# Reordering the rows of a two-stage spectrum so that the real/imaginary exchange copies neighbouring partitions

## The chip, the core and the metric

The kernel runs on one core of one Trainium2 chip. The metric is device time in microseconds of one execution of the whole program. Beside it there is a profile of one execution: busy times of the engines (PE is TensorE, DVE is VectorE, ACT is ScalarE, POOL is GpSimd, SP is SyncE, which here only issues transfers), the DMA queues, and the waits between them.

## The reference

The inputs are bfloat16, one sequence of S = 2048 positions with D = 640 channels. The reference computes a gated long convolution beside a feed-forward block:

```
xn = layernorm(A_q)
kv = (4-tap causal filter of A_k with A_shift_k) * A_v
y  = causal convolution of kv with A_ssm_k along S, per channel   (in the reference by FFT of length 2S)
y  = y + kv * A_ssm_D
s  = xn * y
g  = silu(gelu(xn @ B_w1 + B_b1) @ B_w2 + B_b2)                  (inner width F = 1728)
out = A_q + s * g
```

## The kernel before

**The convolution** is done in the frequency domain with matmuls, in two stages each way. Position s is split as p (128 partitions) and n (16). Stage F1 (`k_f1`, `u_f1`, lines 429 and 442) multiplies each of the 16 slices n by a cosine and a sine matrix (`WA`, `WB`), so that 32 tiles of [128, 640] come out, 128 values r for each n and for each of c = 0, 1. They are stored to DRAM scratch (`k_store` and `u_store`, lines 439 and 449, issued on POOL) and read back in another order (`kin_load` line 479, `uin_load` line 515, issued on SP), so that one tile holds, on its 128 partitions, 4 values of r with all 16 n and both c. Stage F2 (`k_f2` line 482, `u_f2` line 523) multiplies such a tile by one 128x128 matrix `F2m`. What comes out are 32 groups g, each with 128 spectrum rows: 4 values of r, 16 frequencies n, and real or imaginary part c. For the filter the 32 groups are kept in SBUF as `Khat[:, g, :]`. For the signal they stay in PSUM as `mu`.

**The complex product** needs, beside the filter's row, the row with real and imaginary part exchanged. `swap_load(g2)` (line 518, step `mk`) makes it for two groups at a time: two transfers from SBUF to SBUF, issued on SP, copy one half of the spectrum rows of `Khat` onto the other half of the partitions of a ring slot, and back. Before the change c is the highest bit of the row number (row = 64 c + 16 r + n), so the halves are partitions 0 to 63 and 64 to 127. The ring is `Khat` rows 32 to 39, which is four slots of two groups. `product(g)` (line 526, step `mp`) is one VectorE instruction: it multiplies `mu` by `Khat[:, g]` and by the exchanged rows. `inv1` (line 533, step `mc`) turns both products back with the matrices `I1a` and `I1b`, `inv1_out` (`me`) evicts the result, `c_store` (`ms`, POOL) and `cab_load` (`yl`, SP) reorder it through DRAM, and `inv2` (`y`) finishes.

**The three small matrices** `F2m`, `I1a`, `I1b` are made on the chip. `small_iotas` (line 248, step `sp`) writes index vectors on POOL. `small_phase` (line 262, step `s`) takes index bits of the partition number with `bits()` (a bitwise AND and a cast, two VectorE instructions each) and builds phases and masks. `small_sine` (step `ss`) takes the sine on ACT, and `small_mats` (step `sm`) multiplies by the mask.

**The feed-forward block** is tiled by 512 positions (4 chunks): `ffn1` (step `h`, line 376) and `ffn2` (step `g`, line 394) on PE, evictions `he` (line 383) and `ge` on ACT.

**The order** of everything is written out by hand: `PLAN` (line 30) lists the steps, and each engine's instructions and each queue's transfers stand in that order. SP issues the loads `ml` and `mk` in the order of the plan: mk0, ml0, ml1, mk1, mk2, mk3, ml2, ml3, ml5, ml4, ml7, ml10, ml8, mk4, mk5, ml12, ml11, mk6, ml6, mk7, ml9, mk8 to mk10, ml14, ml15, mk11, ml13, mk12 to mk15. A load waits on SP until its ring slot is free, and what is behind it on SP waits too. Near the start, the plan has `sp s A0 h0 h1 P2 ee A1 P1 P0 pt pb he0 he1 h2`: the small phase, the first two `ffn1` groups, the parameter loads, the transposition of the biases (`pt`, line 506) and its eviction (`pb`, line 510), and then the first GELU, which needs the biases. PSUM has two buffers for the feed-forward block, so `h2` waits for `he0`.

Of the kernel before, what the change touches and what calls it, by code (L numbers as in the profile page):

```python
# [14 lines left out]
ALU = mybir.AluOpType  # L15

P = 128
# [57 lines left out]
def kernel(  # L75
# [15 lines left out]
    nc = tc.nc  # L91
# [49 lines left out]
    Khat = wts.tile([P, NG + NR, D], BF16, name="Khat")  # L141
# [65 lines left out]
    def scratch(shape, dtype):  # L207
        n = 1
        for d in shape:
            n *= d  # L210
        reg = next(r for r in regions if r[1] + n <= r[0].shape[1])
        o = reg[1]
        reg[1] += n
        v = reg[0][:, o:o + n]
        if dtype != F32:
            v = v.bitcast(dtype)
        if len(shape) == 2:
            v = v.rearrange("p (a b) -> p a b", a=shape[0])
        elif len(shape) == 3:
            v = v.rearrange("p (a b c) -> p a b c", a=shape[0], b=shape[1])  # L220
        return v
# [24 lines left out]
    sm = {}  # L246

    def small_iotas():
        kcol = scratch([1], I32)
        nc.gpsimd.iota(kcol, pattern=[[0, 1]], base=0, channel_multiplier=1)  # L250

        def grid(*pattern):
            g = scratch([P], F32)
            nc.gpsimd.iota(g, pattern=[list(p) for p in pattern], base=0, channel_multiplier=0,
                           allow_small_or_imprecise_dtypes=True)
            return g

        sm["f"] = grid([0, 8], [1, 16]), grid([8, 2], [0, 64]), grid([0, 2], [32, 4], [0, 16])
        sm["i"] = grid([0, 4], [2, 16], [0, 2]), grid([0, 64], [8, 2]), grid([16, 4], [0, 32])
        sm["kcol"] = kcol  # L260

    def small_phase():
        def bits(mask):
            i = scratch([1], I32)
            nc.vector.tensor_single_scalar(out=i, in_=sm["kcol"], scalar=mask, op=ALU.bitwise_and)
            f = scratch([1], F32)
            nc.vector.tensor_copy(out=f, in_=i)
            return f

        def stt(o, a, s, b, op0, op1):  # L270
            nc.vector.scalar_tensor_tensor(out=o, in0=a, scalar=s, in1=b, op0=op0, op1=op1)

        ph = scratch([3, P], F32)
        mask = scratch([3, P], F32)
        nf, cf, rf = bits(30), bits(1), bits(96)
        ni, ci, ri = bits(15), bits(64), bits(48)
        nm_f, cm_f, rm_f = sm["f"]
        nm_i, cm_i, rm_i = sm["i"]
        c8 = scratch([1], F32)
        nc.vector.tensor_single_scalar(out=c8, in_=cf, scalar=8.0, op=ALU.mult)  # L280
        c4 = scratch([1], F32)
        nc.vector.tensor_single_scalar(out=c4, in_=ci, scalar=0.25, op=ALU.mult)
        stt(ph[:, 0, :], nm_f, nf[:, 0:1], cm_f, ALU.mult, ALU.add)
        stt(ph[:, 2, :], nm_i, ni[:, 0:1], cm_i, ALU.mult, ALU.subtract)
        nc.vector.tensor_scalar(out=ph[:, 1, :], in0=ph[:, 2, :], scalar1=c4[:, 0:1], scalar2=None, op0=ALU.add)
        nc.vector.tensor_scalar(out=ph[:, 2, :], in0=ph[:, 2, :], scalar1=8.0, scalar2=None, op0=ALU.add)
        nc.vector.tensor_scalar(out=ph[:, 0, :], in0=ph[:, 0, :], scalar1=c8[:, 0:1], scalar2=None, op0=ALU.subtract)
        nc.vector.tensor_scalar(out=mask[:, 0, :], in0=rm_f, scalar1=rf[:, 0:1], scalar2=None, op0=ALU.is_equal)
        for i in (1, 2):
            nc.vector.tensor_scalar(out=mask[:, i, :], in0=rm_i, scalar1=ri[:, 0:1], scalar2=2.0 / 4096.0,  # L290
                                    op0=ALU.is_equal, op1=ALU.mult)
        q = scratch([3, P], I32)
        nc.vector.tensor_single_scalar(out=q, in_=ph, scalar=float(8 + 16 + 128), op=ALU.add)
        nc.vector.tensor_single_scalar(out=q, in_=q, scalar=31, op=ALU.bitwise_and)
        sm.update(q=q, sn=scratch([3, P], F32), mask=mask)
# [22 lines left out]
    def take(key, pool, shape, dtype, tag, bufs=None):  # L318
        if key not in live:
            live[key] = pool.tile(shape, dtype, tag=tag, name="%s%d" % key, **({"bufs": bufs} if bufs else {}))  # L320
        return live[key]
# [196 lines left out]
    def swap_load(g2):  # L518
        ks = take(("ks", g2), pools["ring"], None, None, "ks")
        for a in range(2):  # L520
            nc.sync.dma_start(out=ks[64 * a:64 * a + 64, :, :], in_=Khat[64 - 64 * a:128 - 64 * a, 2 * g2:2 * g2 + 2, :])

    def u_f2(g):
        mm2(big_of(("mu", g)), F2m, live["uin", g // 2][:, g % 2, :])
# [48 lines left out]
    def prologue():  # L573
# [92 lines left out]
        "h": ffn1, "he": ffn1_out, "g": ffn2, "ge": ffn2_silu, "gm": ffn2_mul, "ga": last_add, "gs": last_store,  # L666
        "w": f1_phase, "ws": f1_sines, "d": add_d, "em": tap3, "ee": tap3_out,
        "sp": small_iotas, "s": small_phase, "ss": small_sine, "sm": small_mats,
        "kt": k_tr, "kc": k_tr_out, "kf": k_f1, "ke": k_f1_out, "ks": k_store,
        "cv": kv_step, "uf": u_f1, "ue": u_f1_out, "us": u_store,  # L670
        "fl": kin_load, "ff": k_f2, "fe": k_f2_out, "it": i2_tr, "ie": i2_out,
        "ml": uin_load, "mk": swap_load, "mu": u_f2, "mp": product, "mc": inv1, "me": inv1_out, "ms": c_store,
        "q": xq_load, "yl": cab_load, "y": inv2, "yt": gate, "yo": out_add, "ys": out_store,
    }
# [35 lines left out]
```

## Time and profile before

| what | value |
|---|---|
| median of 3 runs | 231.27 us (229.96, 231.27, 231.30) |
| span of the profiled execution, first to last instruction | 231.0 us (no time of its own is listed beside it) |
| PE busy | 211.6 us, 92% |
| DVE busy | 184.1 us, 80% |
| ACT busy | 149.6 us, 65% |
| POOL busy | 43.1 us, 19% |
| the 32 transfers of `swap_load` (160 KB each), issue to landing | min 2.5, median 4.2, max 8.8 us |
| the 32 products on DVE | 1481 ns each, from 119.5 to 175.4 us of the span |

Busy time is read as a share of the span; it is an average over stages that have different limits. Which engine or transfer sets the time in one stage is read from the waits of that stage. A matmul's row shows when it ran, and the granted clock (PEclk) shows how fast TensorE was allowed to run.

### The profile page before, as it was taken

How to read it: one execution, taken by the hardware profiler on the slowest of the kernel's cores; microseconds unless marked ns; L12 is line 12 of the kernel's file. 1: busy time of each engine (PE TensorE's matmuls, PEld its weight loads, DVE VectorE, ACT ScalarE, POOL GpSimd, SP SyncE). 2: the span in 40 equal slices, each digit the busy share in tenths (PEclk: the TensorE clock that was granted, in tenths of full speed). 3: DMA queues.
4: the chain of work that ended last, by engine and by line, in shares of the span. 5: the costliest groups of instructions: out<-in, count | busy, mean ns of one | idle time of the engine just before them, and what ended most of it. 6: DMA issues, size and time to landing. Idle time of an engine off the chain costs nothing.

```text
span 231.0 us, 3921 instructions
## 1 busy us (share of the span) xinstructions
PE 211.6 (92%) x1420; PEld 131.7 (57%) x1420; DVE 184.1 (80%) x315; ACT 149.6 (65%) x232; POOL 43.1 (19%) x75
## 2 busy tenths in 40 slices
PE   7859999899999899979999965999999999999993
PEld 4524456677555556646765532556677765457772
DVE  7799999889989999999779885699998115444892
ACT  3934687998988999898468742567782244562111
POOL 8100020042232344120200220212222000100010
PEclk9988999999999999999999997999999999999999
DMA  7999995654844479599779999877943695379323
GB/s 219 349 380 355 409 413 206 191 209 174 305 191 188 179 236 381 176 309 337 266 215 294 303 353 295 257 231 188 270 156 131 207 340 200 150 218 367 124 89 114
DMA packets 25209, 57.61 MB, mean 249 GB/s; under 512 B 2854, under 2 KB 14055, under 8 KB 25190
## 3 DMA queue, kind: packets, MB, share of 16 engines
q1 hardware_dynamic: 20726, 39.66, 52.6%
q0 software_dynamic: 4320, 17.70, 20.5%
q8 instruction: 11, 0.18, 0.3%
q14 instruction: 8, 0.07, 0.1%
q10 hardware_dynamic: 144, 0.01, 0.0%
HBM read 33.76 MB, written 18.35 MB: 226 GB/s over the span
## 4 chain that ended last, share of the span: by engine, by line
PE 65%; ACT 12%; DMA 9%; DVE 8%; issue 3%; SPq 1%; DVEq 0%; ACTq 0%
PE g L399 22%; PE h L380 21%; ACT Khat L135 6%; DMA kh<-scrU 6%; PE uf L340 3%; PE mc L537 3%; DMA Khat<-Khat 3%; PE mc L538 2%; PE mu L340 2%; PE kf L340 2%; PE ff L340 2%; PE y L556 2%; PE y L557 2%; DMA skp<-in_A_shift_k_dram 1%; ACT sl L404 1%
## 5 line engine op out<-in xcount | busy, mean ns | idle before, releaser
L380 PE MATMUL h<-xnT,w_sb 128*128 128x512 bf16 x280 | 68.4, 390 | 1.5 <-ACT hT L386 1.2
L399 PE MATMUL g<-w_sb,hT 128*128 128x320 bf16 x448 | 63.7, 299 | 0.6 <-ACT sl L404 0.6
L386 ACT ACTIVATE hT<-h,b_f 128x512 bf16<-128x512 f32 (+1 forms) x56 | 38.3, 690 | 27.3 <-PE h L380 24.2
L399 PEld LDWEIGHTS <-hT 128*128 128x128 bf16 x448 | 43.8, 98 | 18.1 <-issue 0.8
L529 DVE TENSOR_TENSOR p<-mu,Khat 128x1280 bf16<-128x1280 f32 x32 | 45.8, 1484 | 5.4 <-PE mu L340 3.7
L380 PEld LDWEIGHTS <-w_sb 128*128 128x128 bf16 x280 | 27.9, 100 | 31.3 <-issue 4.6
L404 ACT ACTIVATE sl<-g 128x320 bf16<-128x320 f32 x32 | 13.9, 439 | 36.1 <-PE g L399 32.5
L135 ACT CAST c<-mc 128x640 bf16<-128x640 f32 x29 | 19.9, 692 | 8.6 <-PE mc L538 7.9
L544 POOL DMA_DIRECT2D scrC<-c x16 | 11.5, 718 | 56.0 <-ACT c L135 51.8
L409 DVE TENSOR_TENSOR xn<-xn,sl 128x320 bf16<-128x320 bf16 x32 | 10.1, 322 | 14.0 <-ACT sl L404 13.8
L472 DVE TENSOR_TENSOR uc<-uc,kvtmp 128x1280 bf16<-128x1280 bf16 x24 | 19.8, 824 | 0.7
L476 DVE TENSOR_TENSOR kvtmp<-kh,w_exp 128x1280 bf16<-128x1280 bf16 x24 | 19.7, 820 | 0.5
L340 PEld LDWEIGHTS <-mats 128*128 128x128 bf16 x128 | 12.1, 97 | 13.8 <-issue 4.9
L537 PE MATMUL mc<-p,mats 128*128 128x320 bf16 x64 | 18.6, 305 | 1.2 <-DVE p L529 0.7
L538 PE MATMUL mc<-p,mats 128*128 128x320 bf16 x64 | 18.5, 304 | 0.0
L563 DVE TENSOR_TENSOR t<-y,xn 128x640 bf16<-128x640 f32 x12 | 9.8, 820 | 10.4 <-PE y L557 10.3
L135 ACT CAST Khat<-uf 128x640 bf16<-128x640 f32 x26 | 17.0, 697 | 0.4 <-PE uf L340 0.4
L340 PE MATMUL mu<-kh,mats 128*128 128x320 bf16 x64 | 13.5, 300 | 3.7 <-DMA kh<-scrU 2.5
L135 ACT CAST Khat<-ff 128x640 bf16<-128x640 f32 x24 | 15.5, 699 | 0.5 <-PE ff L340 0.4
L135 ACT CAST Khat<-kf 128x640 bf16<-128x640 f32 x22 | 15.1, 711 | 0.3 <-PE kf L340 0.2
L440 POOL DMA_DIRECT2D scrK<-Khat x16 | 8.9, 554 | 31.2 <-ACT Khat L135 16.6
L340 PE MATMUL ff<-kin,mats 128*128 128x320 bf16 x64 | 12.3, 298 | 1.4 <-ACT Khat L135 1.3
(111 smaller groups left out, 269.4 us busy)
## 6 DMA issues: line engine op xcount, KB each, us to landing
scrK<-Khat POOLq DMA_DIRECT2D x16, 320.0 KB, 2.6
scrU<-Khat POOLq DMA_DIRECT2D x16, 320.0 KB, 4.2
kin<-scrK SPq DMA_DIRECT2D x16, 320.0 KB, 4.6
Khat<-Khat SPq DMA_DIRECT2D x32, 160.0 KB, 4.2
kh<-scrU SPq DMA_DIRECT2D x16, 320.0 KB, 5.4
scrC<-c POOLq DMA_DIRECT2D x16, 320.0 KB, 3.9
kh<-scrC SPq DMA_DIRECT2D x16, 320.0 KB, 6.2
kh<-in_A_k_dram SPq DMA_DIRECT2D x4, 640.0 KB, 6.1
```

What stands on the lines that cost most here:

```text
L135: return nc.scalar.copy(out=out_ap, in_=in_ap)
L340: nc.tensor.matmul(out=ps[:, h, 0:HALF], lhsT=lhsT, rhs=rhs[:, h * HALF:(h + 1) * HALF], start=start, stop=stop)
L380: nc.tensor.matmul(out=ps[:, :], lhsT=w1_sb[:, t, ft * P:(ft + 1) * P], rhs=xnT[:, t, :], start=(t == 0), stop=(t == DT - 1))
L386: nc.scalar.activation(out=hT[0:M, ft, :], in_=live["h", i][0:M, :], func=ACT.Gelu_apprx_tanh, bias=b1_f[0:M, ft:ft + 1], scale=1.0)
L399: nc.tensor.matmul(out=ps[:, 0:HALF], lhsT=hT[0:M, ft, q * P:(q + 1) * P], rhs=w2_sb[0:M, ft, hs], start=(ft == 0), stop=(ft == FT - 1))
L404: nc.scalar.activation(out=sl[:], in_=live["g", i][:, 0:HALF], func=ACT.Silu)
L472: nc.vector.tensor_tensor(out=uc[:], in0=uc[:], in1=kvtmp[:], op=ALU.add)
L476: nc.vector.tensor_tensor(out=(kvtmp if s else uc)[:], in0=kh[:, r0:r0 + KC, :], in1=w_exp[:, j:j + 1, :].to_broadcast([P, KC, D]), op=ALU ...
L529: nc.vector.tensor_tensor(out=p[:].rearrange("p k (h c) -> p k h c", h=2), in0=live["mu", g][:, None, :, 0:HALF].to_broadcast([P, 2, 2, HA ...
L537: nc.tensor.matmul(out=psC[:, h, 0:HALF], lhsT=I1a, rhs=p[:, 0, hs], start=True, stop=False)
L538: nc.tensor.matmul(out=psC[:, h, 0:HALF], lhsT=I1b, rhs=p[:, 1, hs], start=False, stop=True)
L544: nc.gpsimd.dma_start(out=pair_view(scrC)[g2], in_=live["c", g2][:])
```

## The change

The rows of the spectrum are numbered with c as the lowest bit: row = 32 r + 2 n + c, in place of 64 c + 16 r + n. This is also the order in which the tiles of the DRAM scratch have their rows, so one set of three index vectors serves both directions where there were two sets. `small_iotas` writes three grids in place of six, `small_phase` takes three index values in place of six, and the scratch vectors behind them lie elsewhere in the same regions. The exchange in `swap_load` now copies odd partitions to even ones and even ones to odd ones; each of its two transfers still has 64 rows of 2560 bytes. Matmuls, products, loads, stores and the plan are the same.

```
@@ small_iotas
-        sm["f"] = grid([0, 8], [1, 16]), grid([8, 2], [0, 64]), grid([0, 2], [32, 4], [0, 16])
-        sm["i"] = grid([0, 4], [2, 16], [0, 2]), grid([0, 64], [8, 2]), grid([16, 4], [0, 32])
+        sm["cols"] = grid([0, 4], [1, 16], [0, 2]), grid([0, 64], [8, 2]), grid([32, 4], [0, 32])
@@ small_phase
-        nf, cf, rf = bits(30), bits(1), bits(96)
-        ni, ci, ri = bits(15), bits(64), bits(48)
-        nm_f, cm_f, rm_f = sm["f"]
-        nm_i, cm_i, rm_i = sm["i"]
+        n_in, c_in, r_in = bits(30), bits(1), bits(96)
+        n_out, c_out, r_out = sm["cols"]
         c8 = scratch([1], F32)
-        nc.vector.tensor_single_scalar(out=c8, in_=cf, scalar=8.0, op=ALU.mult)
+        nc.vector.tensor_single_scalar(out=c8, in_=c_in, scalar=8.0, op=ALU.mult)
         c4 = scratch([1], F32)
-        nc.vector.tensor_single_scalar(out=c4, in_=ci, scalar=0.25, op=ALU.mult)
-        stt(ph[:, 0, :], nm_f, nf[:, 0:1], cm_f, ALU.mult, ALU.add)
-        stt(ph[:, 2, :], nm_i, ni[:, 0:1], cm_i, ALU.mult, ALU.subtract)
+        nc.vector.tensor_single_scalar(out=c4, in_=c_in, scalar=16.0, op=ALU.mult)
+        stt(ph[:, 0, :], n_out, n_in[:, 0:1], c_out, ALU.mult, ALU.add)
+        stt(ph[:, 2, :], n_out, n_in[:, 0:1], c_out, ALU.mult, ALU.subtract)
...
-        nc.vector.tensor_scalar(out=mask[:, 0, :], in0=rm_f, scalar1=rf[:, 0:1], scalar2=None, op0=ALU.is_equal)
+        nc.vector.tensor_scalar(out=mask[:, 0, :], in0=r_out, scalar1=r_in[:, 0:1], scalar2=None, op0=ALU.is_equal)
         for i in (1, 2):
-            nc.vector.tensor_scalar(out=mask[:, i, :], in0=rm_i, scalar1=ri[:, 0:1], scalar2=2.0 / 4096.0,
+            nc.vector.tensor_scalar(out=mask[:, i, :], in0=r_out, scalar1=r_in[:, 0:1], scalar2=2.0 / 4096.0,
                                     op0=ALU.is_equal, op1=ALU.mult)
@@ swap_load
         for a in range(2):
-            nc.sync.dma_start(out=ks[64 * a:64 * a + 64, :, :], in_=Khat[64 - 64 * a:128 - 64 * a, 2 * g2:2 * g2 + 2, :])
+            nc.sync.dma_start(out=ks[a:P:2, :, :], in_=Khat[1 - a:P:2, 2 * g2:2 * g2 + 2, :])
```

## The prediction

> **What bounds the kernel now.** I read the page's slices first, for the stage in which PE is not full.
>
> ```profile
> span 231.0 us, 3921 instructions
> PE   7859999899999899979999965999999999999993
> PEclk9988999999999999999999997999999999999999
> DMA  7999995654844479599779999877943695379323
> ```
>
> A slice is 5.8 us. PE is at nine tenths or more nearly everywhere. The gaps are in the first 17 us and in slices 24 and 25 (133 to 144 us), where DMA stands at 9. This is where the exchange (`mk`) runs. The chain of waits for that stretch (start, duration, what):
>
> ```profile
> 122.30 4.67 DMA kh<-scrU
> ...
> 126.99 5.86 DMA Khat<-Khat
> ...
> 133.27 8.10 DMA kh<-scrU
> ...
> 141.42 0.78 PE mu L340 x4
> ```
>
> From 122 to 141 us the path is transfers: loads of the signal's tiles (`ml`, kh<-scrU) and exchanges (`mk`, Khat<-Khat). The load at 133.27 is ml6. It takes 8.10 us, where the fastest of these loads takes 3.4, so 4.7 us of it is queueing behind earlier transfers. PE idles 2.54 us for it (waits: mu L340 from DMA kh<-scrU), and DVE idles 1.5 us at 133.5 for an exchange. The windows of that stage (busy us of PE, PEld, DVE, ACT, POOL, then granted clock, DMA share, GB/s):
>
> ```profile
> 120.00:122.00 2.00, 2.00 (x14) 1.18 (x13) 1.59 (x2) 1.98 (x3) 0.00 (x0) 1.00 1.05 256
> 124.00:126.00 2.00, 1.92 (x13) 0.99 (x11) 1.99 (x3) 1.64 (x3) 0.00 (x0) 1.00 1.12 360
> 131.70:135.11 3.41, 2.25 (x14) 1.16 (x13) 1.82 (x2) 2.38 (x4) 0.71 (x1) 1.00 1.06 362
> 138.53:141.94 3.41, 0.87 (x7) 0.42 (x6) 0.99 (x1) 0.69 (x1) 0.00 (x0) 1.00 1.05 332
> 141.94:145.35 3.41, 3.41 (x12) 1.51 (x10) 2.89 (x2) 0.69 (x1) 0.71 (x1) 0.50 0.77 206
> ```
>
> Three things are to be seen. The 16 DMA engines are saturated (share 1.0 and more) from 118 to 144 us. At the same share, the stretch with exchanges alone (120 to 122) moves 256 GB/s and the one with `ml` alone 360. And after PE's idle time TensorE gets half clock for 3.41 us: five `ffn1` matmuls take 2.13 us at 143.27 and 1.08 at 147.24. The same happens from 15.64 to 19.06, after a stretch in which PE was 43% busy. Stretches with 66% (2.25 of 3.41) and more were not followed by it.
>
> How long a packet lasts, from the DMA view of two short windows, 120 to 122 us (exchanges alone) and 183 to 186 us (the `yl` loads, the same 2560-byte packets, but over 128 partitions):
>
> ```profile
> DMA packets 247, 0.51 MB, mean 256 GB/s; under 512 B 49, under 2 KB 49, under 8 KB 246
> q1 hardware_dynamic: 246, 0.50, 104.5%
> ...
> DMA packets 425, 0.98 MB, mean 326 GB/s; under 512 B 43, under 2 KB 43, under 8 KB 425
> q1 hardware_dynamic: 425, 0.98, 91.1%
> ```
>
> First window: 16 engines x 2 us x 1.045 = 33.4 us for 197 data packets, 0.17 us each. Second: 16 x 3 x 0.911 = 43.7 us for 382, 0.114 us. By the packet records, the 2048 exchange packets have a mean of 160 ns and two lumps, at 102 and near 200. The `yl` packets have a median of 102 and a mean of 123. So about half of the exchange packets run at half rate, as if two engines shared something that engines of a 128-partition load do not share.
>
> The start, by the timelines of DVE and then ACT:
>
> ```profile
> 12.19 0.14 DVE L265 TENSOR_SCALAR GB<-GB 128x1 int32<-128x1 int32 x1
> 12.37 0.15 DVE L267 CAST GB<-GB 128x1 f32<-128x1 int32 x1
> ...
> 15.11 0.17 DVE L512 CAST b_f<-pt 128x14 f32<-128x14 bf16 x1
> ...
> 15.31 1.27 ACT L386 ACTIVATE hT<-h,b_f 128x512 bf16<-128x512 f32 x2 [2.91 <-DVE b_f L512]
> ```
>
> The first GELU waits 2.91 us for the biases, whose eviction stands on DVE behind `small_phase`.
>
> **The change part by part.** The profiled span is 231.04 us, 0.23 below the median of 231.27. I sum on the span and add 0.23.
>
> *Three `bits()` fewer.* The six pairs start 0.25 us apart (10.95, 11.20, ..., 12.44), so DVE reaches L512 0.75 us sooner, at 14.36. But `pt` runs on PE from 14.66 to 14.83, since it waits for its parameter load. So L512 starts at 14.86 in place of 15.11, and PE's next matmul 0.25 us earlier. This falls into the half-clock stretch, so 0.12 us of full-speed time is won. Ends: 0 and 0.75 (all of DVE's lead kept). I take 0.12, since PE's row is the nearest.
>
> *Three iotas fewer on POOL* (0.42 us each, 1.25 us). Hidden: the last one ends at 6.80, its reader on DVE starts at 10.95, and POOL's next work is at 46.27. Without that cover of 4.1 us the gain would be at most the 1.25.
>
> *Scratch vectors elsewhere, matrices with permuted rows.* Same instructions, sizes and order; the regions are overwritten only after `small_mats` (71 us). 0.
>
> *The exchange transfers.* As many as before, as long, at the same place on SP. Issuing one takes 461 to 668 ns today; if that moved by 0.1 us, the 12 exchange transfers from mk1 to mk6 would shift ml6 by 1.2 us on SP, which its 4.7 us of queueing covers. What can change is the duration of a packet. Ahead of ml6 in the saturated queue are mk1 to mk6, 768 packets with a mean of 154 ns: 768 x 154 / 16 = 7.4 us of all engines. Each ns of that mean moves ml6 by 0.048 us. Bounds below: 102 ns gives -2.5 us, 123 (the `yl` loads) -1.5. Bounds above: 204 (always at half rate) +2.4, 247 (the slowest twentieth of these packets today) +4.5. [...] So I take 140, about half way from 154 to 123: -0.7 us.
>
> *What is late next.* From 145 to 177 us PE is busy 31.7 of 32 us, so time won before 141.42 is kept. The exchanges after mk7 lie beside that full PE and give nothing; uncovered, their 1024 packets would be worth 0.064 us for each ns.
>
> *The half clock.* With ml6 0.7 us earlier, PE idles 1.9 us there, and that stretch would be about 46% busy. This is nearer to the 43% that was halved than to the 66% that was not, so I leave the half-clock stretch in. Worth if it goes: 3.41 / 2 = 1.7 us.
>
> Sum: 231.04 - 0.12 - 0.7 = 230.2, with 0.23 added 230.4.
>
> **The rivals.**
>
> *The packets lose their half rate altogether.* At the `yl` loads' 123 ns ml6 lands 1.5 us earlier, PE idles about 1 us and is 70% busy in that stretch, so the half clock goes too: 231.27 - 0.12 - 1.5 - 1.7 = 227.9; at 102 ns 227.0. For it: the lump at 102, and that 128-partition transfers show none near 200. Against it: half the rows of all partitions are not all rows. [...]
>
> *Reading and writing meet (the other side).* Today each transfer reads in one half of the partitions and writes in the other. Afterwards each row's source is its destination's neighbour, so the place that gives is also the one that takes. If these hinder each other, packets get longer. At 247 ns: 231.27 - 0.12 + 4.5 = 235.6. It decides (over 1%) from about 205 ns on. For it: only these transfers have both ends in SBUF, and only they are slow. Against it: from 132 to 136 us stores and loads run side by side, and the loads keep 55 to 57 ns for 1280 bytes.
>
> *The second transfer waits for the first.* If the tracking of dependencies takes every second partition for the whole range, the two transfers into one slot seem to overlap, and SP waits for the first to land, with all later `ml` behind it: 2.5 us at least in place of 0.6, for six pairs ahead of ml6 11 us, less the 4.7 of queueing 6.7; with the median landing (4.2) 17. I take 12: 243. Against it: the product at 119.54 reads rows 0 and 32 of `Khat` in one stepped view, and ACT writes row 26 while it runs (third of the casts from 118.83 to 120.73), so steps along a row are followed exactly.
>
> *Nothing changes in the packets* is the forecast's upper end, 231.2.
>
> **How the numbers follow.** Forecast (packets 125 to 154 ns): 0.46, own range 229.0 to 231.3. Full rate: 0.27. Reading meets writing: 0.14, of which 0.02 stays within 1%. The wait: 0.08. Unforeseen and slower: 0.05. About 1% (2.3 us) is what a measurement of this kernel can tell from no change. Faster 0.27, same 0.46 + 0.02 = 0.48, slower 0.12 + 0.08 + 0.05 = 0.25. The range goes from 227.3, near the full-rate end, to 235.8, just over the 235.6; left out are the wait and most of the unforeseen (0.12) and the tails of the full-rate case and of the meeting (0.07).
>
> **What would show it.** Exchange packets near 140 ns, the rate in an exchange-only stretch near 290 GB/s in place of 256, ml6's landing at about 140.5 with PE's idle time near 1.9 us, L512 at 14.9. Wrong would be: packets at 102 to 123 with no half clock after the exchange; packets over 200; or SP standing between the two transfers of a pair until the first has landed.

## The result, and the profile after

The changed kernel takes 228.4 us in the median of 17 runs (226.47 to 231.81), the kernel before on the same chip 232.02 (17 runs). The ratio is 0.9869, with a 95% interval of 0.9831 to 0.9907: 1.3% faster. This ratio and those of the experiments leave out executions over 1.5% above their kernel's fastest, so this one is a little nearer to 1 than the ratio of the means over all runs, 0.984.

The slices of the page after, to be held against those shown before:

```profile
span 225.2 us, 3912 instructions
PE   7869989899999899979999988999999999999993
PEclk9999999999999999999999999999999999999999
DMA  6999996645844469599849999866833694389223
```

The gap of PE in slices 24 and 25 is nearly gone (8 and 8 tenths, where 6 and 5 stood), and no slice has a lowered clock. This execution's time is 226.99 us, 1.8 above its span. So 1.8 us lie around the span, where the prediction counted 0.2.

The windows of the exchange stage after (columns as before), first a stretch with exchanges alone, then the two clock windows in which ml6 landed:

```profile
118.00:120.00 2.00, 2.00 (x14) 1.14 (x13) 1.74 (x2) 1.98 (x3) 0.00 (x0) 1.00 0.89 335
...
133.28:136.70 3.42, 2.50 (x15) 1.25 (x14) 3.29 (x3) 2.07 (x3) 0.72 (x1) 1.00 1.04 401
136.70:140.11 3.41, 3.13 (x24) 1.87 (x23) 2.61 (x2) 1.69 (x3) 0.71 (x1) 1.00 0.90 339
```

The exchanges alone move 335 GB/s with the engines 89% busy, where before they moved 256 at 105%. PE is 73% and 92% busy in the two windows, and the clock stays full. The wait for ml6, in PE's timeline after:

```profile
136.28 0.86 PE L337 MATMUL mu<-kh,mats 128*128 128x320 bf16 x4 [0.35 <-DMA kh<-scrU]
```

It is 0.35 us where it was 2.54, and it ends at 136.28 in place of 141.42. By the packet records, an exchange packet now lasts 105.3 ns in the mean of mk1 to mk6 (154.4 before), and 2% last over 150 ns (58% before). In SP's timeline the six transfers of mk1 to mk3 are issued without a stop, and the start is earlier as reckoned (PE, then DVE):

```profile
115.55 3.96 SPq L518 DMA_DIRECT2D Khat<-Khat  x6
```

```profile
14.64 0.17 PE L505 MATMUL pt<-ident,prm 19*128 19x19 bf16 x1 [0.76 <-DMA prm<-in_B_b_dram]
15.79 1.46 PE L377 MATMUL h<-xnT,w_sb 128*128 128x512 bf16 x6 [0.98 <-ACT hT L383]
...
14.84 0.17 DVE L509 CAST b_f<-pt 128x14 f32<-128x14 bf16 x1
```

The eviction of the biases follows `pt`, no longer `small_phase`, and PE goes on at 15.79 in place of 16.05.

For most executions the mean granted clock is on record (not for the 17 of the kernel before that the ratio above rests on). Over all of these, of both kernels:

| granted clock | before: runs, mean us | after: runs, mean us |
|---|---|---|
| 0.995 and more (no half-clock stretch while PE works) | 12, 229.86 | 10, 227.20 |
| 0.987 to 0.994 (one) | 17, 232.15 | 12, 229.02 |
| under 0.987 (two or more) | 18, 233.70 | 1, 231.81 |
| all | 47, 232.16 | 23, 228.35 |

The number of half-clock stretches in the first column is what the 14 profiles of this study show at such clocks, apart from one that begins in the last 6 us of a program. So the gain has two parts. At equal clock it is 2.7 us. The rest of the 3.8 us between the means is clock: (1 - clock) x time falls from 2.58 to 1.33 us in the mean, and in both kernels a microsecond of it goes with 0.92 us of time (a straight line through each kernel's runs), which is 1.2 us.

### The profile page after: what moved, and what is told of

Same layout as the page of the kernel before. It is cut to its first block, busy times and chain, and to the rows that moved or that the text cites. A ratio compares the mean times of both kernels' runs of the same rounds, so it can differ in the third digit from the quotient of the medians.

```text
span 225.2 us, 3912 instructions
## 1 busy us (share of the span) xinstructions
PE 209.3 (93%) x1420; PEld 131.5 (58%) x1420; DVE 183.2 (81%) x309; ACT 149.7 (66%) x232; POOL 42.5 (19%) x72
## 4 chain that ended last, share of the span: by engine, by line
PE 59%; issue 13%; ACT 11%; DVE 7%; DMA 7%; SPq 1%; POOL 1%; DVEq 0%; POOLq 0%; ACTq 0%
PE g L396 20%; PE h L377 20%; ACT Khat L135 5%; DMA prm<-in_B_b_dram 4%; PE uf L337 3%; PE mc L534 2%; DMA scrC<-c 2%; PE mc L535 2%; PE kf L337 2%; PE mu L337 2%; PE y L553 2%; PE y L554 2%; DVE p L526 2%; DVE Khat L136 2%; PE ff L337 1%
## 5 line engine op out<-in xcount | busy, mean ns | idle before, releaser
L377 PE MATMUL h<-xnT,w_sb 128*128 128x512 bf16 x280 | 65.8, 379 | 1.3 <-ACT hT L383 1.0
L377 PEld LDWEIGHTS <-w_sb 128*128 128x128 bf16 x280 | 27.3, 98 | 29.3 <-issue 1.5
L534 PE MATMUL mc<-p,mats 128*128 128x320 bf16 x64 | 18.1, 298 | 1.6 <-DVE p L526 1.1
L535 PE MATMUL mc<-p,mats 128*128 128x320 bf16 x64 | 18.1, 298 | 0.0
```

The source lines that it names most:

```text
L377: nc.tensor.matmul(out=ps[:, :], lhsT=w1_sb[:, t, ft * P:(ft + 1) * P], rhs=xnT[:, t, :], start=(t == 0), stop=(t == DT - 1))
L534: nc.tensor.matmul(out=psC[:, h, 0:HALF], lhsT=I1a, rhs=p[:, 0, hs], start=True, stop=False)
L535: nc.tensor.matmul(out=psC[:, h, 0:HALF], lhsT=I1b, rhs=p[:, 1, hs], start=False, stop=True)
```

## The experiments

My theory after the result (T) was that the gain comes from the exchange packets; rival M was the shorter start. Two kernels have one part of the change each.

**Transfers alone** (kernel before):

```
-            nc.sync.dma_start(out=ks[64 * a:64 * a + 64, :, :], in_=Khat[64 - 64 * a:128 - 64 * a, 2 * g2:2 * g2 + 2, :])
+            nc.sync.dma_start(out=ks[a:P:2, :, :], in_=Khat[1 - a:P:2, 2 * g2:2 * g2 + 2, :])
```

> The kernel before with the new odd/even transfers alone; the matrices keep the old row order, so the product gets wrong rows, and only the time counts. Theory T (the gain comes from faster exchange packets): packets near 105 ns, ratio to before 0.987 to 0.990, nearly the whole change. Rival M (the gain comes from the shorter start): packets near 105 ns all the same, but a ratio of 0.997 to 1.000.

Measured: 229.33 us, ratio to the kernel before 0.9894 (0.9848 to 0.9941), packets of mk1 to mk6 104.6 ns.

**Matrices alone** (changed kernel, with the old line in `swap_load`):

```
-            nc.sync.dma_start(out=ks[a:P:2, :, :], in_=Khat[1 - a:P:2, 2 * g2:2 * g2 + 2, :])
+            nc.sync.dma_start(out=ks[64 * a:64 * a + 64, :, :], in_=Khat[64 - 64 * a:128 - 64 * a, 2 * g2:2 * g2 + 2, :])
```

> The changed kernel with the old half-to-half transfers; here too the product gets wrong rows, and only the time counts. Theory T: packets near 155 to 160 ns and a ratio to before of 0.997 to 1.000, the 0.1 to 0.25 us of the start. Rival M: 0.987 to 0.990.

Measured: 231.58 us, ratio 0.9979 (0.9936 to 1.0022), packets 152.0 ns. The two ratios multiply to 0.987, the whole change. Theory T holds. The start's part is of the size that was reckoned, but this measurement cannot tell it from zero.

**Why half to half is slow.** Theory H, which rests on the two lumps at 102 and near 200 ns: 64 neighbouring partitions of one half leave two engines sharing something. Rival X: the rows cross from one half to the other.

```
-            nc.sync.dma_start(out=ks[a:P:2, :, :], in_=Khat[1 - a:P:2, 2 * g2:2 * g2 + 2, :])
+            nc.sync.dma_start(out=ks[64 * a:64 * a + 64, :, :], in_=Khat[64 * a:64 * a + 64, 2 * g2:2 * g2 + 2, :])
```

> The changed kernel, where each half of the partitions is copied onto itself in place of odd onto even (no exchange is made; the rows of the product are wrong). Theory H (64 neighbouring partitions leave engines sharing a part of SBUF, whichever way the rows go): packets still in two lumps, mean 145 to 175 ns. Rival X (packets are slow because the rows cross from one half to the other): one lump, mean 102 to 112 ns.

Measured: packets 149.9 ns (mk1 to mk6), 54% over 150 ns; the one run took 231.67 us. Nothing crosses, and it is as slow. Rival X falls.

**Which end.** One kernel writes halves and reads every second partition, the other the reverse:

```
+            nc.sync.dma_start(out=ks[64 * a:64 * a + 64, :, :], in_=Khat[1 - a:P:2, 2 * g2:2 * g2 + 2, :])
...
+            nc.sync.dma_start(out=ks[a:P:2, :, :], in_=Khat[64 - 64 * a:128 - 64 * a, 2 * g2:2 * g2 + 2, :])
```

> The changed kernel, where each transfer reads odd (or even) partitions and writes one half (rows land in the wrong place). It tells which end is slow. If engines meet where they write: mean 145 to 175 ns; if only where they read: 102 to 112 ns. Theory H says nothing on the end; rival X would give something between, since half of the rows cross.

> The changed kernel, where each transfer reads one half and writes odd (or even) partitions (wrong rows). The counterpart of the run that writes halves: if engines meet where they read, mean 145 to 175 ns; if only where they write, 102 to 112 ns.

Measured: with halves written 156.2 ns over all exchanges (50% over 150 ns), with halves read 145.8 (35%). Neither end alone is free, so the either-or of my expectations was wrong: both ends slow the packets. Which end costs more is not settled. In mk1 to mk6 it is the writing end (175.6 against 129.4 ns), in mk12 to mk15 the reading end (192 against 165). In time, the single run with halves written took 231.58 us at a clock of 0.991, the one with halves read 228.19 at 0.997, which is the order of their packets in mk1 to mk6.

**One transfer in place of two:**

```
-        for a in range(2):
-            nc.sync.dma_start(out=ks[a:P:2, :, :], in_=Khat[1 - a:P:2, 2 * g2:2 * g2 + 2, :])
+        nc.sync.dma_start(out=ks[:, :, :], in_=Khat[:, 2 * g2:2 * g2 + 2, :])
```

> The changed kernel with one transfer of 128 partitions in place of two of 64 (rows are copied without an exchange, so the product is wrong). Theory H: packets near 105 ns as with odd and even, and a time within 0.4% of the changed kernel's, since SP's 16 issues fewer are not on the path. If splitting into two transfers costs something itself, the time is lower by over 0.5%.

Measured: 228.33 us, ratio 0.9864 (0.9772 to 0.9955), packets of mk1 to mk6 107.9 ns. In their packets, odd and even together are as good as one transfer over all partitions. Its four runs all have a clock of 0.999 or more and a mean of 228.14 us, where the changed kernel has 227.20 at a clock of 0.995 and more: at equal clock the single transfer is no faster, and rather slower. Why is not shown.

**The step of two inside one half:**

```
-            nc.sync.dma_start(out=ks[a:P:2, :, :], in_=Khat[1 - a:P:2, 2 * g2:2 * g2 + 2, :])
+        for lo in (0, 64):
+            for a in range(2):
+                nc.sync.dma_start(out=ks[lo + a:lo + 64:2, :, :], in_=Khat[lo + 1 - a:lo + 64:2, 2 * g2:2 * g2 + 2, :])
```

> The changed kernel with the same exchange as four transfers: odd and even partitions of the lower half, then of the upper half (32 rows each; the result is the reference's). Theory H: the step of two is not what helps, the reach over both halves is; inside one half packets are slow again, 145 to 175 ns, and the time goes back towards that of before (0.995 to 1.003). If it is the step of two that helps: packets 102 to 115 ns, and a ratio near 0.988 unless the 32 more issues on SP cost something.

Measured: packets of mk1 to mk6 142.8 ns (41% over 150), and 235.98 us, ratio 1.0178 (1.0071 to 1.0286). The packets came out nearly as theory H said, just under its 145: the step does not help inside a half. The time I missed; SP's timeline shows why (SPq marks the issuing of transfers), this run first, then the kernel before:

```profile
118.02 7.74 SPq L519 DMA_DIRECT2D Khat<-Khat  x12
125.81 3.69 SPq L513 DMA_DIRECT2D kh<-scrU  x7
129.59 6.88 SPq L519 DMA_DIRECT2D Khat<-Khat  x8
...
140.33 0.54 SPq L513 DMA_DIRECT2D kh<-scrU  x1
```

```profile
117.14 3.94 SPq L521 DMA_DIRECT2D Khat<-Khat  x6
...
133.27 0.54 SPq L516 DMA_DIRECT2D kh<-scrU  x1
```

Twelve issues take 7.74 us where six took 3.94, and ml6 is issued at 140.33 in place of 133.27. The packets are not slower than those of the kernel before (154.4 ns), so what is added goes with the issues: twice the transfers is too much for SP's queue here.

**Is it any 64 neighbours?** Each exchange is one transfer, of the middle partitions or of the lower half:

```
-        for a in range(2):
-            nc.sync.dma_start(out=ks[a:P:2, :, :], in_=Khat[1 - a:P:2, 2 * g2:2 * g2 + 2, :])
+        lo = 0 if g2 % 2 else 32
+        nc.sync.dma_start(out=ks[lo:lo + 64, :, :], in_=Khat[lo:lo + 64, 2 * g2:2 * g2 + 2, :])
```

> The changed kernel, where every exchange is one transfer of 64 neighbouring partitions onto themselves: partitions 32 to 95 for even numbers of the exchange, 0 to 63 for odd ones (no exchange is made and half of the slot stays stale, so the product is wrong). [...] If any 64 neighbouring partitions are slow: both in two lumps.

The windows of three exchanges that run by themselves: mk12 (partitions 32 to 95), mk13 (0 to 63), mk14 (32 to 95). The last two columns are the DMA share and GB/s:

```profile
149.70:150.30 0.60, 0.60 (x5) 0.26 (x3) 0.60 (x2) 0.60 (x1) 0.00 (x0) 1.00 0.71 273
152.40:153.40 1.00, 1.00 (x9) 0.68 (x8) 0.48 (x2) 0.98 (x2) 0.18 (x1) 1.00 0.76 164
153.90:154.50 0.60, 0.60 (x5) 0.32 (x4) 0.60 (x1) 0.60 (x1) 0.60 (x2) 1.00 0.73 273
```

At about the same share the middle moves 273 GB/s and the half 164. By the packet records mk12 to mk15 have means of 105, 188, 108 and 200 ns. Earlier, where exchanges queue close together, the split is less clean: mk2 (the middle) came out at 177 ns between mk1 and mk3, and mk7 (a half) at 110. Over all sixteen the middle has 118 and the half 178. The one run took 227.65 us. So in these windows 64 neighbours are not slow as such, only when they lie in one half (0 to 63). Why, no run shows.

**What the exchange still costs:**

```
-        for a in range(2):
-            nc.sync.dma_start(out=ks[a:P:2, :, :], in_=Khat[1 - a:P:2, 2 * g2:2 * g2 + 2, :])
```

> The changed kernel without the exchange transfers (the product reads what lies in the ring slots). It shows what the exchange still costs after the change. My reading: PE is busy 91% from 121 to 145 us after the change, 2.1 us idle in 24; without 13 us of packets on 16 engines ml6 lands earlier and at most those 2 us are won, ratio to before 0.975 to 0.985. If the exchange is already free: 0.985 to 0.989.

Measured: 226.63 us, ratio 0.9808 (0.9729 to 0.9887). At a clock of 0.995 and more it has 226.15 us (two runs) against 227.20 of the changed kernel: about 1 us is left.

**The half clock by itself** (theory K). The kernel before gets nine idle matmuls ahead of the one that waits for ml6:

```
-... mk8 mk9 mc8 me8.a mc10 me10.a mu12 mp12 ...
+... mk8 mk9 mc8 me8.a mc10 me10.a fi9 mu12 mp12 ...
+    def fill(n):
+        pf = ps_ffn.tile([P, 512], F32, tag="ffn", name="pf%d" % n)
+        for _ in range(n):
+            nc.tensor.matmul(out=pf[:].rearrange("p (a b) -> p a b", a=4), lhsT=ident[:],
+                             rhs=ident[:, None, :].to_broadcast([P, 4, P]), start=True, stop=True)
```

> The kernel before with nine more 128x512 matmuls on PE (1.9 us at full clock, their result is not used) just ahead of the matmul that waited for ml6 at 141.42; the transfers are the old ones. Theory K (part of the gain is the half clock that follows PE's idle time there): the extra work hides in the 2.5 us of idle time, the half-clock stretch near 142 us goes in most executions, and the time falls by 0.5 to 1.5 us, ratio 0.993 to 0.998. If the half clock costs nothing of its own: ratio 0.999 to 1.003, or more where the extra work is not hidden.

Measured: 232.51 us, ratio 1.0052 (1.0009 to 1.0095). The clock did as expected, since none of 12 executions is under 0.987 (6 of the 17 of the kernel before beside them). The time did not: by clock the runs stand at 230.44 (two) and 232.46 us (ten), 0.3 to 0.6 above the kernel before. The added work costs about what the clock returns: over all runs the means are 232.12 and 232.10 us. As a proof of the half clock's price this run is a miss.

**The start filled** (changed kernel; `fb` is `fill` with a PSUM tile of the other pool):

```
-... A1 P1 P0 pt pb he0 he1 h2 ...
+... A1 P1 P0 fb3 pt pb fb4 he0 he1 h2 ...
```

> The changed kernel with seven more matmuls (results not used) in PE's two idle places near 14 and 15 us, around the transposition of the biases. Theory K: the half-clock stretch that begins between 15 and 18 us in about half of the executions of the changed kernel goes, and the mean falls by 0.5 to 1.0 us, ratio to before 0.983 to 0.986. If the clock does not follow PE's busy share there, the ratio stays at 0.987 or goes up.

The timeline of PE:

```profile
13.57 0.81 PE L663 MATMUL pb<-ident 128*128 128x512 bf16 x3
15.20 0.17 PE L505 MATMUL pt<-ident,prm 19*128 19x19 bf16 x1 [0.82 <-DMA prm<-in_B_b_dram]
15.30 1.04 PE L663 MATMUL pb<-ident 128*128 128x512 bf16 x4
```

> The changed kernel again, on the same chip as the two with more matmuls, so that they can be set against it: ratio to before 0.983 to 0.991, granted clock 1.0 in about half of the executions.

Measured on the same chip: 227.15 us (226.78 to 228.19), ratio 0.9841 (0.9783 to 0.9899), against 228.59 (226.63 to 229.99), ratio 0.9879 (0.9806 to 0.9951) of the changed kernel again. All six filled runs have a clock of 0.997 or more; of the changed kernel's six, four have 0.989 to 0.993. The means are 227.27 and 228.44 us. The intervals overlap, so that this version beats the changed kernel is likely, not shown; that the half clock at the start goes is shown.

## Why the prediction was right and wrong

The time lies in the range, and the sign is right. But it was not the forecast (230.4) that came true: it was the rival in which the packets lose their half rate altogether (227.9 predicted, 228.4 measured). The time is in the range because the range reached down to that rival. That 227.9 and 228.4 lie so close is partly luck: the rival took 1.5 us for the packets, 1.7 for the clock and 0.12 for the start, and the runs give 2.7 at equal clock and 1.2 for the clock.

- **What bounds the kernel**: right. ml6's place behind the exchanges set PE's idle time, and it moved with the packets. Two readings were slightly off, without effect on the sum: from 126 to 128 us the DMA share is 0.95, and POOL's next work after the iotas is at 33.25 us, not 46.27.
- **The packet's duration**: this step failed. "So I take 140" has 105 in its place. By 0.048 us for each ns that is 2.4 us in place of 0.7. No run shows the 140, a guess about half way between two measured means (154 and 123 ns); with odd and even rows the runs showed 105.3 ns (changed kernel) and 104.6 (transfers alone). How the rows of a transfer are dealt to the engines no trace shows. The guess was worth less than the two lumps: the packets then took the lower one, at 102 ns.
- **A term that was missing**: from the issue of ml0 to the end of the wait for ml6 the stage is 3.5 us shorter (116.13 to 141.42 before, 114.53 to 136.28 after), and the packets explain 2.4. Other packets beside the exchanges got shorter too. From the issue of mk1 to the end of that wait, the loads' packets last 65.9 ns before and 62.7 after, the stores' 221.5 and 201.4. That is 3100 x 3.2 / 16 = 0.6 us and 200 x 20 / 16 = 0.3 us, 3.3 us with the 2.4. The stores' difference is steady: 222 to 232 ns with the old transfers (kernel before, matrices alone, nine matmuls more) and 201 to 203 with the new ones (changed kernel, changed kernel again, start filled, transfers alone). The loads' is less so: 64.6 to 68.2 against 61.6 to 63.5. That slow exchange packets hold up the others is argued from this, not shown, and the sum fits this pair of profiles only: between matrices alone and transfers alone the stage differs by 2.3 us.
- **The half clock**: left in by the forecast at 46% busy, gone at 73%. As a decision on the packets it fell with them. That it can go was in the rival, at 1.7 us; one stretch less goes with 1.6 to 2.3 us in the table (the single run with two after the change left aside). In the mean the clock's whole part of the gain is 1.2 us; 12 of the 47 runs of the kernel before have no such stretch at all.
- **The start**: 0.25 us earlier, as reckoned; what it is worth in time the runs cannot tell from zero.
- **The wait of the second transfer, and reading against writing**: neither is there. SP issues the three pairs of mk1 to mk3 without a stop (3.96 us for the six, 3.94 before), and with neighbouring source and destination the packets last 105.3 ns, near the lower lump at 102.
- **The sum against the median**: 0.23 us were added to the span where 1.8 lie around it. The profiled execution of before had two half-clock stretches; its time, about 232.8 us with these 1.8, was longer than the three beside whose median it was set.

What stays open: which engine gets which rows of a 64-row transfer, whether engines share anything at all, as theory H has it, and so why the packets of odd and even rows hardly ever last over 150 ns (2%).

## What to carry to other kernels

In a stage where the transfers are saturated, look at the duration of single packets, and not only at bytes: here a fast lump at 102 ns and a slow one near 200 went with transfers inside one half of the partitions. Lay out an exchange so that each of its transfers reaches both halves of the partitions; every second partition (105.3 ns a packet, 154.4 before) and the middle 64 (105 and 108 ns, the lower half 188 and 200, in mk12 to mk15) did here; do not pay for it with more transfers on a full queue (twelve issues took 7.74 us where six took 3.94). And where PE's idle time leaves a 3.41 us window of the clock 43% busy or less, as in the 12 windows counted below, count a half-clock stretch beside it (1.6 to 2.3 us in the table); at 49% and more none followed here.

## What the runs showed of the hardware

In the profiles of this study the half clock goes with a sharp condition. In each profile all stretches lie on one grid of 3.413 us, whose place against the program differs from profile to profile. Over the 14 profiles of this study, leaving aside the last 6 us of each program, all 12 windows of that grid in which PE was busy 43% or less (0.13 to 0.43) were followed by a window at half clock, and every window with 49% or more by one at full clock. A window did not have to be idle: the 43% of 12.23 to 15.64 us in the kernel before was already too little. Whether a short idle time halves the clock differs between executions of one kernel: by the granted clock, 12, 17 and 18 of the 47 runs of the kernel before stand in the table's three rows, with means of 229.9, 232.2 and 233.7 us, a spread as large as the change's gain. The grid's place is one possible reason, which no run here isolates. The changed kernel's two profiles show another one: their grids lie 0.1 us apart, but the transposition of the biases waits 0.76 us in the one shown above and 1.44 in the other (changed kernel again):

```profile
15.55 0.17 PE L505 MATMUL pt<-ident,prm 19*128 19x19 bf16 x1 [1.44 <-issue]
```

The window with this wait is 49% busy in the first and 29% in the second, and only the second is followed by half clock.
